# A transformer block with adaptive layer norm on one core: one of four x tiles loaded on two queues, and the 1 of the first scale added by TensorE

## The chip, the core and the metric

The kernel runs on one core of a Trainium2 chip. The metric is the device time of one execution in microseconds; runs of a kernel are compared by their median.

## What is computed

The inputs are bf16. x is 2 x 256 x 1152 (B, N, D), c is 2 x 1152, and the weights have D rows.

```python
def reference(x, c, wqkv, wo, w_mod):
    B, N, D = x.shape
    mod = (_silu(c) @ w_mod).reshape(B, 6, 1, D)
    shift_a, scale_a, gate_a, shift_m, scale_m, gate_m = [mod[:, i] for i in range(6)]
    h = _layernorm(x, axis=-1) * (1 + scale_a) + shift_a
    qkv = h @ wqkv
    ...
    p = _softmax(jnp.einsum('bqd,bkd->bqk', q, k) * D ** (-0.5), axis=-1)
    a = jnp.einsum('bqk,bkd->bqd', p, v) @ wo
    return x + gate_a * a
```

Three of the six parts of `mod` are used: the scale and the shift ahead of the projections, and the gate behind the output projection.

## The kernel before

The 512 tokens (both batches) lie in TT = 4 tiles of P = 128 rows, tiles 0 and 1 of the first batch and 2 and 3 of the second. D = 1152 is cut into KT = 9 blocks of 128.

**Layer norm in pieces.** Each x tile is centred by its mean (`centre`, into `xc`), and TensorE transposes the centred tile block by block (`transposes`, into the PSUM tiles `tp`); VectorE and ScalarE copy the result to `xcT` (`xcT_copy`). The division by the standard deviation comes later, so the K projection can begin before the variances are known. The mean of tile 0 comes from VectorE (`bn`), those of tiles 1 and 2 from sums on ScalarE (`act_mean`), that of tile 3 from both.

**Scale.** The scale row is silu(c) times a part of w_mod (`wS`). It is made in four column parts: PA (blocks 0 and 1), PB (2 to 4), PC (5 and 6), PD (7 and 8). For PA, `scale_rows` multiplies 128 x 128 blocks of `wS` with the replicated silu(c) (`scT_rep`, 32 columns) into the PSUM tile `psS`: 8 small matmuls for kk = 0 to 3 and 10 for kk = 4 to 8, each group behind a load of its own. Then `scale_out` adds 1 and writes `s1p` to SBUF, and `scaled` and `scaled_tp` multiply the transposed x by it into `hTs`.

**K projection.** `k_part`, `pair_part` and `k_step` accumulate wK against `hTs` in PSUM, block by block of k as the weights arrive: `acc` holds five of the nine output blocks, `psE` pairs of the others for the first two k, and `psK` the others for the rest. The shift (`wH`, into `psH`, by `shift_tiles`) is made after most of K, the third part of its weights last. Then come Q, the scores, V, the attention and the output projection.

**In front.** As x and the first weights arrive, TensorE runs `fillers(12)`: twelve matmuls of the constant tile `junk` (all ones, 512 columns) whose result nobody reads.

**Order.** Every engine's instructions run in the order in which they are written: lists for each engine are pinned at the end (`pin`). All large loads are issued on SP in a written order: x tiles 0, 1, 2, two loads of `wS` for PA, wK(0), x tile 3, wK(1), two loads of `wS` for PB, wK(2) to wK(4), and so on to `wH`, wQ, wG, wV and wO. ScalarE issues the small load of c on its own queue, and the last store. Each DMA takes one of eight semaphores in turn, and so waits for the DMA that had it before. Where nothing else is said, a DMA's landing is the sixteenth increment of its semaphore.

The change touches these lines of the main sequence (351, 366 to 372):

```python
    fillers(12)
    ...
    scale_rows(PA, 0, 4, where=BA)
    centre(2, nmean[:, 2:3], ALU.add)
    xcT_copy(1, 0, True)
    xcT_copy(1, 1, False)
    scale_rows(PA, 4, KT, js=[(0, 1), (1, 2)])
    scale_out(PA)
    scaled_b(0, 0)
    transposes(2, 0, BB)
```

`BA`, `BB` and `BC` name single PSUM banks; `scaled_b(0, 0)` is `scaled` for block 0 and the first batch. In the profile nearly all instructions stand under line 85, that of the helper that records them, so groups are told apart by their tiles.

Of the kernel before, what the change touches and what calls it, by code (L numbers as in the profile page):

```python
# [11 lines left out]
BF16 = mybir.dt.bfloat16  # L12
# [4 lines left out]
def kernel(  # L17
# [10 lines left out]
    P = 128  # L28
    B, N, D = x.shape
    T = B * N  # L30
    KT = D // P
# [9 lines left out]
    PA, PB, PC, PD = (0, 2), (2, 5), (5, 7), (7, KT)  # L41
    KA = PA[1]
    NR = 32

    x_f = x.rearrange("b n d -> (b n) d")
# [10 lines left out]
    const = ctx.enter_context(tc.tile_pool(name="const", bufs=1))  # L56
# [5 lines left out]
    MM, BA, BB, BC = (psum, "mm"), (psum_a, "pa"), (psum_b, "pb"), (psum_c, "pc")  # L62
# [3 lines left out]
    def bank(shape, name, dtype=None, where=None):  # L66
        if where is None:
            where = ring[turn_no[0] % len(ring)]
            turn_no[0] += 1
        return where[0].tile(shape, dtype or F32, tag=where[1], name=name)  # L70
# [21 lines left out]
    vec = _Rec(nc.vector, dve_seq)  # L92
    sca = _Rec(nc.scalar, act_seq)
    ten = _Rec(nc.tensor, pe_seq)
    spq = _Rec(nc.sync, sp_seq)
    gps = _Rec(nc.gpsimd, pool_seq)
# [10 lines left out]
    def tok(b):  # L107
        return slice(b * N, (b + 1) * N)

    def one(t):  # L110
        return slice(t * P, (t + 1) * P)

    junk = const.tile([P, 512], BF16)
# [4 lines left out]
        out=ident, in_=ident, compare_op=ALU.not_equal, fill=1.0, base=0,  # L118
# [9 lines left out]
        out=mask, in_=mask, compare_op=ALU.is_ge, fill=0.0, base=0,  # L128
# [3 lines left out]
        out=mask, in_=mask, compare_op=ALU.is_ge, fill=0.0, base=2,  # L132
# [2 lines left out]

    c_sb = const.tile([P, B, KT], BF16)
    x_sb = act.tile([P, TT, D], BF16)
    sca.preload_act_table_set("natural_log_exp_and_others")
    sca.dma_start(out=c_sb, in_=c.rearrange("b (p k) -> p b k", k=KT))

    wK = wpool.tile([P, KT, D], BF16)
    wQ = wpool.tile([P, KT, D], BF16, name="wQ")
# [4 lines left out]
    def load_x(t):  # L147
        spq.dma_start(out=x_sb[:, t, :], in_=x_f[t * P : (t + 1) * P, :])
# [4 lines left out]
    def load_s(part, k0, k1):  # L153
        load_mod(wS, 1, k0, k1, part[0] * P, part[1] * P)
# [10 lines left out]

    load_x(0)
    load_x(1)
    load_x(2)
    load_s(PA, 0, 4)
    load_s(PA, 4, KT)  # L170
    load_k(0, 1)
# [21 lines left out]
    def fillers(n):  # L193
        for _ in range(n):
            ten.matmul(junk_ps, lhsT=junk[:, :P], rhs=junk, start=True, stop=True)
# [7 lines left out]
    def sc_rhs(kk):  # L203
        return scT_rep[:, kk].rearrange("p r b -> p (r b)")
# [35 lines left out]
    def centre(t, scalar, op, c0=0, c1=D):  # L240
        vec.tensor_scalar(out=xc[:, t, c0:c1], in0=x_sb[:, t, c0:c1], scalar1=scalar, scalar2=None, op0=op)
# [4 lines left out]
    def transposes(t, h, where):  # L246
        k0, k1 = HALF[h]
        tp = bank([P, 5, P], "tp", BF16, where)
        for k in range(k0, k1):
            ten.transpose(tp[:, k - k0, :], xc[:, t, k * P : (k + 1) * P], ident)  # L250
        tps[t, h] = tp
# [9 lines left out]
    s1p = const.tile([P, KT, B], F32)  # L261
# [5 lines left out]

    psS = {}

    def scale_rows(part, kk0, kk1, js=None, where=None):  # L270
        if kk0 == 0:
            psS[part] = bank([P, part[1] - part[0], NR], "psS", where=where)
        for j0, j1 in [part] if js is None else js:
            for kk in range(kk0, kk1):
                for j in range(j0, j1):
                    ten.matmul(psS[part][:, j - part[0], :], lhsT=wS[:, kk, j * P : (j + 1) * P], rhs=sc_rhs(kk),
                               start=(kk == 0 and j == part[0]), stop=(kk == KT - 1), skip_group_check=True)

    def scale_out(part):
        vec.tensor_scalar_add(out=s1p[:, part[0] : part[1], :], in0=psS[part][:, :, 0:B], scalar1=1.0)  # L280
# [17 lines left out]
    def scaled(k, sl, scalar):  # L298
        vec.tensor_scalar(out=hTs[:, k, sl], in0=xcT[:, k, sl], scalar1=scalar, scalar2=None, op0=ALU.mult)
# [5 lines left out]
    def scaled_b(k, b):  # L305
        scaled(k, tok(b), s1p[:, k, b : b + 1])
# [41 lines left out]
        vec.tensor_tensor(out=qkT[:, KT + NACC + i, :], in0=psK[i], in1=held[:, i, :], op=ALU.add)  # L348


    fillers(12)
    sca.activation(out=e_sb, in_=c_sb, func=ACT.Exp, scale=-1.0)
    gps.tensor_scalar_add(out=e_sb, in0=e_sb, scalar1=1.0)
    bn(0, after_second=silu_c)
# [8 lines left out]
    xcT_copy(0, 1, False)  # L363
    transposes(1, 0, MM)
    transposes(1, 1, MM)
    scale_rows(PA, 0, 4, where=BA)
    centre(2, nmean[:, 2:3], ALU.add)
    xcT_copy(1, 0, True)
    xcT_copy(1, 1, False)
    scale_rows(PA, 4, KT, js=[(0, 1), (1, 2)])  # L370
    scale_out(PA)
    scaled_b(0, 0)
    transposes(2, 0, BB)
    transposes(2, 1, BC)
    scaled_tp(0, 2)
# [63 lines left out]
    def scale_part(part):  # L439
        scale_rows(part, 0, KT, where=BB)  # L440
        scale_out(part)
        for k in range(*part):
            for b in range(B):
                scaled_b(k, b)
# [112 lines left out]
    for b in range(B):  # L557
        s_ps = bank([P, NQ, N], "s_ps")
        for i in range(NQ):
            tq = b * NQ + i  # L560
            for k in range(KT):
                ten.matmul(s_ps[:, i, :], lhsT=qkT[:, k, tq * P : (tq + 1) * P], rhs=qkT[:, KT + k, tok(b)],
                           start=(k == 0), stop=(k == KT - 1))
# [75 lines left out]
    for b in range(B):  # L639
        for gi, dv0 in enumerate(range(0, KT, 2)):  # L640
            ndv = min(2, KT - dv0)
            ps = bank([P, 2, N], "ps")
            for dd in range(ndv):
                dv = dv0 + dd
                for j in range(NQ):
                    ten.matmul(ps[:, dd, :], lhsT=v_sb[:, b * NQ + j, dv * P : (dv + 1) * P],
                               rhs=pT_sbs[b][:, j, :], start=(j == 0), stop=(j == NQ - 1))
# [3 lines left out]
    for t in range(TT):  # L651
# [11 lines left out]
        for ci, (c0, w_) in enumerate(chunks):  # L663
# [6 lines left out]
            for k in range(KT):  # L670
                ten.matmul(
                    ps, lhsT=attnT[:, k, t * P : (t + 1) * P],
                    rhs=(wo_last[:, k, c0 - (D - TAILW) : c0 - (D - TAILW) + w_] if pregated else wO[:, k, cs]),
                    start=(k == 0 and not pregated), stop=(k == KT - 1),
# [49 lines left out]
```

## Time and profile before

| what | us |
|---|---|
| median of 3 runs (lowest, highest) | 96.11 (96.08, 96.26) |
| the profiled execution | 96.27 |
| its span, first to last instruction | 94.5 |
| TensorE busy (of the span) | 90.0 (95%) |
| VectorE busy | 69.9 (74%) |
| ScalarE busy | 34.3 (36%) |
| GpSimd busy | 20.4 (22%) |
| loads: bytes read from HBM | 19.76 MB |

PE is TensorE's matmul, PEld its weight load, DVE VectorE, ACT ScalarE, POOL GpSimd and SP the engine that issues the loads. A row of the timeline or of the chain begins with its start and its length in us; `<-` points from what an instruction reads to what it writes, and brackets give the idle time of the engine before it and what ended it. The rows of digits cut the span in 40 equal slices and give tenths. The ends of matmuls are modelled, so their starts are the surer figure.

### The profile page before, as it was taken

To read this page: it belongs to the slowest core of one execution; us is meant where nothing else is said; L and a number is where in the kernel's file an instruction comes from. 1 tells how busy PE (TensorE), PEld (TensorE's weight loads), DVE (VectorE), ACT (ScalarE), POOL (GpSimd) and SP (SyncE) were. 2 spreads that over 40 slices of the span, in tenths; PEclk is the share of its full clock that TensorE was granted. 3 is DMA by queue.
4 is the path that set the end of the run, shared out by engine and by line. 5 is a ranking of instruction groups with operands and counts; after the bars stand their busy time and mean duration, and the time that the engine had idled before them with its cause. 6 is when DMAs were issued, how large, how long until landed. Compare 5 with 4: busy or idle time off the path is not lost.

```text
span 94.5 us, 1687 instructions
## 1 busy us (share of the span) xinstructions
PE 90.0 (95%) x664; PEld 52.9 (56%) x664; DVE 69.9 (74%) x133; ACT 34.3 (36%) x71; POOL 20.4 (22%) x24
## 2 busy tenths in 40 slices
PE   3999999999999999999999999999999999999970
PEld 1349884543445444444468656565678665665660
DVE  2478889245898977999999899991018487889970
ACT  5198688002462700093420589234246300000010
POOL 5521000800000000000000000007999990002000
PEclk9999999999999999999999999999999999999999
DMA  1999999999999999999999702200000000302203
GB/s 25 321 275 378 373 400 358 365 393 407 398 410 412 411 410 412 401 375 365 380 410 411 285 18 56 54 9 0 0 0 0 0 0 7 125 34 91 105 26 118
DMA packets 17207, 21.31 MB, mean 225 GB/s; under 512 B 2224, under 2 KB 10544, under 8 KB 17200
## 3 DMA queue, kind: packets, MB, share of 16 engines
q1 hardware_dynamic: 16784, 21.17, 61.7%
q10 hardware_dynamic: 416, 0.04, 0.3%
q8 instruction: 5, 0.08, 0.3%
q14 instruction: 2, 0.02, 0.0%
HBM read 19.76 MB, written 1.18 MB: 222 GB/s over the span
## 4 chain that ended last, share of the span: by engine, by line
PE 93%; DVE 3%; issue 0%
PE ps L85 40%; PE psQ L85 18%; PE acc L85 11%; PE psK L85 7%; PE junk_ps L85 6%; PE s_ps L85 4%; PE psS L85 2%; PE tp L85 2%; PE psE L85 2%; PE psH L85 1%; DVE o_sb L85 1%; DVE ga L85 1%; DVE junk L85 1%; PE bc_ps L85 0%; DVE hTs L85 0%
## 5 line engine op out<-in xcount | busy, mean ns | idle before, releaser
L85 POOL PARTITION_ALL_REDUCE gate_bc<-gacc x2 | 13.7, 6886 | 45.2 <-DVE gacc L85 45.2
L85 DVE SCALAR_TENSOR_TENSOR gacc<-wG,scT_f,gacc 128x1152 f32<-128x1152 bf16 x16 | 22.4, 1416 | 0.4
L85 PE MATMUL ps<-wV,hT 128*128 128x384 bf16 x108 | 17.7, 326 | 0.0
L85 PE MATMUL psQ<-hT,wQ 128*128 128x512 bf16 x81 | 17.6, 379 | 0.0
L85 PE MATMUL ps<-wO,attnT 128*128 128x384 bf16 (+1 forms) x108 | 17.2, 322 | 0.0
L85 PEld LDWEIGHTS <-attnT 128*128 128x128 bf16 x117 | 11.1, 98 | 6.5
L85 PEld LDWEIGHTS <-hT 128*128 128x128 bf16 x108 | 10.6, 98 | 6.9
L85 PEld LDWEIGHTS <-wK 128*128 128x128 bf16 x109 | 9.3, 98 | 7.3 <-issue 0.6
L85 PEld LDWEIGHTS <-wQ 128*128 128x128 bf16 x81 | 7.9, 98 | 9.6
L85 PE MATMUL acc<-hTs,wK 128*128 128x512 bf16 (+2 forms) x65 | 11.3, 314 | 0.1
L85 ACT CAST qkT<-psQ 128x512 bf16<-128x512 f32 x9 | 4.9, 597 | 11.1 <-PE psQ L85 11.1
L85 DVE TENSOR_TENSOR ga<-ps,gate_bc 128x384 f32<-128x384 f32 (+1 forms) x12 | 6.5, 544 | 2.9 <-PE ps L85 2.9
L85 DVE CAST attnT<-ps 128x512 bf16<-128x512 f32 (+1 forms) x6 | 3.5, 603 | 6.8 <-PE ps L85 6.8
L85 ACT CAST v_sb<-ps 128x384 bf16<-128x384 f32 x12 | 5.5, 476 | 7.9 <-PE ps L85 7.9
L85 PE MATMUL psK<-hTs,wK 128*128 128x512 bf16 x28 | 6.9, 380 | 0.0
L85 DVE TENSOR_TENSOR o_sb<-ga,x_sb 128x384 bf16<-128x384 f32 (+1 forms) x12 | 6.6, 547 | 0.4
L85 PE MATMUL junk_ps<-junk 128*128 128x512 bf16 x12 | 5.3, 629 | 1.5 <-DVE junk L85 1.5
L85 ACT CAST o_sb<-ps 128x128 bf16<-128x128 f32 x1 | 0.3, 265 | 17.3 <-PE ps L85 17.3
L85 DVE TENSOR_TENSOR hT<-hTs,held 128x512 bf16<-128x512 bf16 x9 | 5.8, 686 | 0.9 <-ACT held L85 0.9
L85 DVE BATCH_NORM_STATS2 stats<-x_sb 128x6 f32<-128x384 bf16 x6 | 3.1, 542 | 2.3 <-DMA x_sb<-in_x_dram 2.3
L85 PEld LDWEIGHTS <-junk 128*128 128x128 bf16 (+1 forms) x13 | 1.7, 137 | 4.7 <-issue 3.2
L85 PE MATMUL s_ps<-qkT 128*128 128x256 bf16 x36 | 4.1, 272 | 0.0
(77 smaller groups left out, 84.6 us busy)
## 6 DMA issues: line engine op xcount, KB each, us to landing
wH<-in_w_mod_dram SPq DMA_DIRECT2D x3, 864.0 KB, 8.9
wG<-in_w_mod_dram SPq DMA_DIRECT2D x3, 864.0 KB, 12.3
wV<-in_wqkv_dram SPq DMA_DIRECT2D x3, 864.0 KB, 13.4
wO<-in_wo_dram SPq DMA_DIRECT2D x3, 864.0 KB, 8.8
wK<-in_wqkv_dram SPq DMA_DIRECT2D x7, 288.0 KB, 6.6
wQ<-in_wqkv_dram SPq DMA_DIRECT2D x3, 576.0 KB, 12.2
x_sb<-in_x_dram SPq DMA_DIRECT2D x4, 288.0 KB, 3.6
wS<-in_w_mod_dram SPq DMA_DIRECT2D x3, 320.0 KB, 7.6
```

The lines of the kernel that those rows point to most:

```text
L85: r = fn(*a, **k)
```

## The change

Tile 2 of x is loaded by two DMAs: rows 0 to 103 on SP, in the place of the whole tile, and rows 104 to 127 on ScalarE's queue behind c. One filler is left out. In its place `scale_open` opens the PSUM tile of part PA with a matmul of one row of ones against one row of ones, which writes 1 to each of its 64 columns; the scale matmuls of PA then accumulate on it. The first `scaled` reads its factor from `psS` itself, and `s1p` of PA is a plain copy, made after that `scaled`. The other parts are as before.

```diff
+    ones_row = const.tile([1, 2 * NR], BF16)
+    gps.memset(ones_row, 1.0)
     sca.preload_act_table_set("natural_log_exp_and_others")
     sca.dma_start(out=c_sb, in_=c.rearrange("b (p k) -> p b k", k=KT))
+    XS = 104
+    sca.dma_start(out=x_sb[XS:, 2, :], in_=x_f[2 * P + XS : 3 * P, :])
...
     load_x(0)
     load_x(1)
-    load_x(2)
+    spq.dma_start(out=x_sb[:XS, 2, :], in_=x_f[2 * P : 2 * P + XS, :])
     load_s(PA, 0, 4)
...
+    def scale_open(part, where):
+        n = part[1] - part[0]
+        psS[part] = bank([P, n, NR], "psS", where=where)
+        ten.matmul(psS[part].rearrange("p j r -> p (j r)"), lhsT=junk[0:1, :P], rhs=ones_row[0:1, 0 : n * NR],
+                   start=True, stop=False, skip_group_check=True)
+
     def scale_rows(part, kk0, kk1, js=None, where=None):
-        if kk0 == 0:
+        opened = part == PA
+        if kk0 == 0 and not opened:
             psS[part] = bank([P, part[1] - part[0], NR], "psS", where=where)
...
-                               start=(kk == 0 and j == part[0]), stop=(kk == KT - 1), skip_group_check=True)
+                               start=(kk == 0 and j == part[0] and not opened), stop=(kk == KT - 1),
+                               skip_group_check=True)
...
-    fillers(12)
+    fillers(11)
+    scale_open(PA, BA)
...
-    scale_rows(PA, 0, 4, where=BA)
+    scale_rows(PA, 0, 4)
...
     scale_rows(PA, 4, KT, js=[(0, 1), (1, 2)])
-    scale_out(PA)
-    scaled_b(0, 0)
+    scaled(0, tok(0), psS[PA][:, 0, 0:1])
+    vec.tensor_copy(out=s1p[:, PA[0] : PA[1], :], in_=psS[PA][:, :, 0:B])
     transposes(2, 0, BB)
```

## The prediction

> **What bounds the kernel now.** I read the engine rows and the slices of the page first, then the chain that ended last in order of time, then the front (5.7 to 9.1 us) instruction by instruction in the timeline, and last the stretches with their DMA share and the DMA queues. The page:
>
> ```profile
> PE 90.0 (95%) x664; PEld 52.9 (56%) x664; DVE 69.9 (74%) x133; ACT 34.3 (36%) x71; POOL 20.4 (22%) x24
> ...
> PEclk9999999999999999999999999999999999999999
> DMA  1999999999999999999999702200000000302203
> ```
>
> TensorE is busy from end to end, so the end moves only by what TensorE's stream gains or loses in its few holes. The DMA row is full through the first 22 slices (52 us). The change touches only the first 10 us of instructions, and the loads behind them. The chain there (start, length, what):
>
> ```profile
> 0.96 0.50 DVE junk L85
> 1.46 0.05 issue
> 1.51 5.30 PE junk_ps L85 x12
> 6.81 1.25 PE tp L85 x18
> 8.06 0.46 PE psS L85 x18
> 8.51 0.02 issue
> 8.54 0.17 DVE s1p L85
> 8.71 0.02 issue
> 8.73 0.30 DVE hTs L85
> 9.03 0.04 issue
> 9.07 0.98 PE acc L85 x10
> ```
>
> Twelve constant matmuls, eighteen transposes of tiles 0 and 1, the first scale part, the add of 1 (`s1p`), one scaling (`hTs`), then the K projection without a break. The timeline of the same stretch, then of two later holes:
>
> ```profile
> 6.21 0.11 PEld L85 LDWEIGHTS <-xc 128*128 128x128 bf16 x1 [0.32 <-DVE xc L85]
> ...
> 6.60 1.46 PE L85 MATMUL tp<-ident,xc 128*128 128x128 bf16 x18
> ...
> 8.54 0.16 DVE L85 TENSOR_SCALAR s1p<-psS 128x4 f32<-128x4 f32 x1
> ```
> ```profile
> 10.22 0.22 PEld L85 LDWEIGHTS <-wK 128*128 128x128 bf16 x3 [0.22 <-DMA wK<-in_wqkv_dram]
> ```
> ```profile
> 28.90 0.24 PEld L85 LDWEIGHTS <-scT_rep 128*32 128x32 bf16 x11 [0.17 <-issue]
> ```
>
> The first transpose's operand was there at 6.21 but its matmul started at 6.60, behind the last constant matmul. At 10.22 the weights for k=1 wait for their load. The hole at 28.90 has no releaser named; by the trace the third `wH` load landed at 28.855 and its first matmul started at 28.897. By the spacing of matmul starts, those two holes cost 0.107 and 0.131 us, and no other matmul after 9.1 us waits for a DMA. So the kernel is TensorE's stream held at two places by loads: **wK(1) at 10.2 and wH(third) at 28.9**.
>
> **The front, step by step.** Constant matmuls start 0.426 us apart, so without the twelfth TensorE is free at 6.175. The new one has 64 columns, 64/512 of that: 0.05 (an estimate from that spacing; between 0.03, the spacing of the 32-column psS matmuls, and 0.43), end 6.23. The operand was ready at 6.17, so the transposes start near 6.28, 0.32 earlier. The clock opened at 7.193: transposes are 0.107 apart before and 0.056 after. Eight and a half fit in 6.28 to 7.19, the other nine and a half take 0.53, so psS may start at 7.73, not 7.895. Its second half needs the wS load that landed at 7.95; before, TensorE got to it at 8.075. Now it waits there until about 8.00 and psS ends 8.42 instead of 8.50: 0.08 gained.
>
> Then `s1p` (8.538) goes from in front of the first `hTs` (8.734): 0.196 gained, `hTs` starts near 8.46. VectorE is free for it: `centre(2)` (7.61) waited for a copy that itself waited for the transposes, and can move to 7.40 (the mean is ready at 7.36), the copy after it to 7.83. Reading the factor from PSUM is not in the trace; the nearest row, the 128-column `hTs` from PSUM, takes 0.28 like the 256-column one from SBUF (0.29), so I take 0, and 0.1 as the other end (a gain has no reason). The copy of `s1p` now stands after the first `hTs`, at 8.66 to 8.82; queued behind it is `hTs` of tile 2, done at 9.14, and TensorE wants that only after five matmuls of 0.108, at 9.34: covered by 0.2. The first projection matmul moves from 9.075 to 8.80. **Sum: 0.27 at that point, and nothing at the end yet:** the 1.04 us of work up to wK(1) is then done at 9.84, while wK(1) landed at 10.175. The wait grows from 0.107 to 0.38. So the end is set by when wK(1), and then wH, land.
>
> Small edits, one answer each: `ones_row` (0.10, like the memset of `neg_half`) lies in GpSimd's idle 0.74 before `e_sb`. ScalarE's second DMA issue (0.45, like that of c) ends by 1.8, its next work starts at 3.90. On SP the semaphores shift by one: load_x(3) now waits for tile 0 (3.705, before its 3.857), wK(1)'s issue for tile 1 (4.47, so 0.14 later than its 4.33); it lands 5.8 us after issue behind loads already queued, so 0. From wK(2) on each waits for the same load as before. Tile 1 may land up to 0.18 later where two moved rows slip in front of it. ScalarE's sums start with it (4.47, 4.49), so the mean of tile 2 goes to 7.54, and `centre(2)` to 7.57, still before its old 7.61. Tile 0 late by as much would halve the 0.32.
>
> **The split load.** A 288 KB tile is 128 packets, eight on each of 16 DMA engines; the weight loads of that size landed 0.70 us apart, 0.088 a row. No load of the trace has 104 or 24 rows. Whole shares can leave an engine anything from none to 16 rows of this tile, so -0.70 to +0.70 us on an engine. I take the even shares, 13 engines with 8 and 12 with 2, because every load shown is cut evenly: twelve engines carry 10 rows (+0.18), one 8, three none (-0.70). The Trainium skill says the same of HWDGE transfers (DMA: Bandwidth & Descriptors, "Why a DMA increments its semaphore by 16 and not by 1"): the largest count up to 16 that divides the slowest dimension, on the lowest-numbered engines; no run so far shows it.
>
> Are the +0.18 seen? The stretches (PE, PEld, DVE, ACT, POOL, clock, DMA share, GB/s) and the queues of 13 to 30 us:
>
> ```profile
> 1.00:4.00 3.00, 2.49 (x6) 0.87 (x7) 0.72 (x2) 1.17 (x2) 2.06 (x5) 1.00 0.69 201
> 4.00:7.00 3.00, 3.00 (x11) 1.24 (x10) 2.52 (x7) 2.60 (x6) 0.96 (x3) 1.00 0.95 280
> 7.00:10.00 3.00, 2.94 (x55) 2.75 (x53) 2.61 (x10) 2.57 (x7) 0.24 (x1) 1.00 1.04 373
> ```
> ```profile
> q8 instruction: 2, 0.03, 0.7%
> ```
>
> Between 4 and 7 us the engines are filled to 0.95 where 1.04 follows: 0.27 us an engine unspent, more than two rows. The rows come on a second queue, behind c, just then. I take them as hidden (0), and keep +0.18 as the other end. For wK(1) the sixteen landings ran from 9.46 to 10.18, the four last at 10.06 or later; without the three relieved ones a landing near 10.05 is what I take: -0.12 at the first hole. For the third wH thirteen engines landed by 27.49 and three at 28.07, 28.79 and 28.86. One of the late ones fell 1.5 us behind right after a 16 KB instruction packet at 14.96, another after the one at 24.37: the instruction row. [...] The trace does not name the engines.
>
> **Sum:** -0.12 - 0.131 = -0.25. The profiled execution took 96.27 (span 94.5 and 1.77 around it), so 96.02; it stands 0.16 above the median, which becomes **95.86**. From -0.13 (second hole alone) to -0.33 (0.20 at the first).
>
> **Rivals.** *No change, 96.11:* the late engines of wH are not relieved, the two rows are hidden, and every front gain turns into a longer wait at 28.9. For it: that hole takes up any gain. Against: three late, three relieved. The Trainium skill speaks for this one too (same page, "Rules for kernel authors"): splitting a load over partitions and queues is not worth doing, as both parts share the same 16 engines; the even shares above would contradict it.
>
> *Slower, 96.29:* the twelve engines set the pace. Two rows of 0.088 are not hidden, wK(1) lands at 10.35 and the third wH at 29.03; TensorE waits for both and ends 0.18 later. It decides if the engine that lands last is one of the twelve and the early holes of the queues are not filled. For it: the DMA row is full for 52 us, so nothing is made up later; against: the 0.95.
>
> *Clock late, about 97.3:* a matmul less in front lets the clock open later than 7.19. TensorE's 2.6 us of work from there to 10.2 would at most double; less the 0.38 of waits and half of it again, +1.2. Against: transposes follow the filler without a hole. The Trainium skill (TensorE: Matmul & The Clock Gate, "The HAM clock gate") puts the next opening 3.4 us later if a window is missed; the trace has one opening and cannot show it.
>
> That the 1 is not added on TensorE, or the split not made, is excluded by the order of instructions, which shows both.
>
> **How the numbers follow.** Forecast 0.43, no change 0.24, slower by the twelve engines 0.28, clock 0.05. Range 95.75 to 96.36: the forecast's own is 95.78 to 95.98, the slower case's end 96.29 with 0.07 for a slower read from PSUM and a late tile 0; the clock case is left out. About 0.2% (0.19 us) is what a measurement here can tell from no change. The forecast's -0.25 passes it in a little over nine cases of ten; the slower case's +0.18 stands on it and passes in two of three. Faster 0.40, same 0.36, slower 0.24.
>
> **What would show it.** In the profile after: the first transpose near 6.3 and the first `acc` near 8.8; the wait for wK(1) longer than 0.22, ending near 10.05 if the rows are hidden, 10.35 if not; no hole in front of the third part of `psH` if the late engines are the relieved ones. A first `acc` later than 9.07, or transposes still 0.107 apart after 7.2, would break the front; a wH landing at 28.86 or later breaks the forecast.

## The result: 0.46 us slower, where 0.25 faster was forecast

The changed kernel takes 96.58 us (median of 20 runs, 96.44 to 96.89) against 96.12 (20 runs, 95.87 to 96.65): a ratio of 1.0042, 95% interval 1.0026 to 1.0058. The forecast of 95.86 had the wrong sign, and 96.58 lies above its range. The profiled execution of the changed kernel took 96.51, with a span of 94.8.

The page of the changed kernel shows TensorE busy 1.0 us less than before, the clock full, and the DMA row full through the first 22 slices:

```profile
PE 89.0 (94%) x664; PEld 52.6 (55%) x664; DVE 70.0 (74%) x133; ACT 34.1 (36%) x71; POOL 20.5 (22%) x25
...
PEclk9999999999999999999999999999999999999999
DMA  2999999999999999999999502110000000302203
```

TensorE does less work and ends later, so something holds it. The chain that ended last names it (changed kernel, start, length, what). Before the change this chain ran on TensorE from its first constant matmul on, with `s1p` and one `hTs` as its only steps elsewhere in the front; now it does not touch TensorE until 11.73:

```profile
1.25 3.81 DMA x_sb<-in_x_dram
...
5.08 1.26 ACT xc L85 x2
...
6.47 1.25 ACT xc L85 x2
7.74 0.21 ACT nmean L85
...
7.98 0.52 DVE xc L85
8.50 0.34 DVE xcT L85
...
8.94 0.29 DVE hTs L85
9.23 0.08 DVE s1p L85
...
9.41 0.67 DVE hTs L85 x3
10.08 0.20 DVE xcT L85
10.28 0.60 DVE half L85
...
11.23 0.37 DVE xc L85
11.59 0.14 issue
11.73 0.38 PE tp L85 x4
```

It begins with the load of tile 1 (3.81 us from its issue), goes over ScalarE's sums of tiles 1 and 2 (`xc` on ACT) to the mean of tile 2 at 7.95, over VectorE's `centre(2)`, the copy of tile 1, the four `hTs` with `s1p` among them, the copy of tile 2 and the half sum of tile 3, to the centring of tile 3 and its first transpose. The timeline of the changed kernel gives the two waits in it, and TensorE's starts in front:

```profile
5.08 1.16 ACT L85 ACTIVATE xc<-x_sb 128x1152 bf16<-128x1152 bf16 x1 [0.90 <-DMA x_sb<-in_x_dram]
...
6.20 0.68 PE L85 MATMUL tp<-ident,xc 128*128 128x128 bf16 x9 [0.61 <-DVE xc L85]
...
9.28 0.98 PE L85 MATMUL acc<-hTs,wK 128*128 128x256 bf16 x10
...
11.73 0.38 PE L85 MATMUL tp<-ident,xc 128*128 128x128 bf16 x4 [0.20 <-DVE xc L85]
```

The same two starts before:

```profile
4.49 1.16 ACT L85 ACTIVATE xc<-x_sb 128x1152 bf16<-128x1152 bf16 x1 [0.37 <-DMA x_sb<-in_x_dram]
...
11.28 0.39 PE L85 MATMUL tp<-ident,xc 128*128 128x128 bf16 x4
```

ScalarE's first sum starts at 5.08 where it started at 4.49; the first `acc` starts at 9.28, not at 9.07 as before or 8.80 as forecast; and tile 3's first transpose stands at 11.73, not at 11.28. From there to the first `psH` TensorE loses nothing more: 28.46 against 28.01, again 0.45. The span grew by less, 94.8 against 94.5, since the hole of 0.131 at the third `wH` was in before's profiled execution and is not in this one. That execution lay 0.15 above its kernel's median, so the two medians, 0.46 apart, are what the 0.45 is to be held against. Nothing behind tile 3 moves: in all nineteen profiled executions of this document the time from its first transpose to the end is 84.78 to 84.87, but for before's 85.00 with that hole.

The stretch of 4 to 7 us, with TensorE, its weight loads, VectorE, ScalarE, GpSimd, clock, DMA share and GB/s, in which I had counted on 0.27 us an engine of unspent DMA time:

```profile
4.00:7.00 3.00, 2.26 (x16) 1.04 (x14) 2.47 (x7) 2.07 (x5) 0.96 (x3) 1.00 1.08 289
```

The share rose from 0.95 to 1.08, by 14%, and the bytes from 280 to 289 GB/s, by 3%. The engines were busier, but with longer packets: rows of 2304 bytes, 0.093 us each on an undisturbed engine, took 0.155 on average between 4.50 and 5.00.

### The profile page after: what moved, and what is told of

Same layout as the page of the kernel before. It is cut to its first block, busy times and chain, and to the rows that moved or that the text cites. A ratio compares the mean times of both kernels' runs of the same rounds, so it can differ in the third digit from the quotient of the medians.

```text
span 94.8 us, 1692 instructions
## 1 busy us (share of the span) xinstructions
PE 89.0 (94%) x664; PEld 52.6 (55%) x664; DVE 70.0 (74%) x133; ACT 34.1 (36%) x71; POOL 20.5 (22%) x25
## 4 chain that ended last, share of the span: by engine, by line
PE 83%; DVE 5%; DMA 4%; ACT 3%; issue 1%; SPq 0%; DVEq 0%
PE ps L85 40%; PE psQ L85 18%; PE acc L85 9%; PE psK L85 7%; PE s_ps L85 4%; DMA x_sb<-in_x_dram 4%; ACT xc L85 3%; PE psS L85 1%; PE psE L85 1%; PE psH L85 1%; DVE o_sb L85 1%; DVE hTs L85 1%; DVE ga L85 1%; DVE xc L85 1%; PE tp L85 1%
## 5 line engine op out<-in xcount | busy, mean ns | idle before, releaser
L85 PE MATMUL junk_ps<-junk 128*128 128x512 bf16 x11 | 4.0, 532 | 1.5 <-DVE junk L85 1.5
L85 PE MATMUL tp<-ident,xc 128*128 128x128 bf16 x36 | 2.9, 220 | 1.4 <-DVE xc L85 1.4
L85 PE MATMUL ps<-pT,v_sb 128*128 128x256 bf16 x36 | 4.1, 272 | 0.0
```

Source lines behind the costliest of these rows:

```text
L85: r = fn(*a, **k)
```

## The experiments

"Tile 1 lands" is the sixteenth increment of its load, "mean" the end of ScalarE's mean of tile 2, "tile 3" the start of its first transpose; all come from the profiled execution of the kernel named. Before has 4.47, 7.36 and 11.28; the changed kernel 5.05, 7.95 and 11.73. The theory after the comparison: the 24 rows on ScalarE's queue make tile 1 late, and `s1p`, in its new place, lengthens VectorE's work behind that. The rivals: one of the two halves of the change does it all; the uneven shares of 104 and 24 rows do it; the slip is in tile 2 itself.

### The halves

**The edits without the split.** The changed kernel with tile 2 loaded whole on SP:

```diff
-    XS = 104
-    sca.dma_start(out=x_sb[XS:, 2, :], in_=x_f[2 * P + XS : 3 * P, :])
...
-    spq.dma_start(out=x_sb[:XS, 2, :], in_=x_f[2 * P : 2 * P + XS, :])
+    load_x(2)
```

> The three TensorE and VectorE edits alone (one filler less, the 1 added on TensorE, the copy of s1p behind the first hTs); tile 2 of x whole on SP. If the split load is what costs: tile 1 lands near 4.47 us as before, the wait behind tile 3's chain is gone, and the time is that of before or a little less, 95.95 to 96.15. If the edits cost by themselves (the copy of s1p holds up VectorE, the filler is missed): 96.4 to 96.6 with tile 1 on time.

Measured: 96.11 against 96.15, ratio 1.0004 (0.9985 to 1.0023). Tile 1 lands at 4.43. The timeline of this kernel:

```profile
8.46 0.29 DVE L85 TENSOR_SCALAR hTs<-xcT,psS 128x256 bf16<-128x256 bf16 x1
...
8.80 0.98 PE L85 MATMUL acc<-hTs,wK 128*128 128x256 bf16 x10
...
10.19 1.05 PEld L85 LDWEIGHTS <-wK 128*128 128x128 bf16 x12 [0.39 <-DMA wK<-in_wqkv_dram]
```

and the piece of its chain that follows:

```profile
4.25 5.91 DMA wK<-in_wqkv_dram
10.15 0.04 issue
10.20 0.72 PE acc L85 x5
```

The first `hTs` at 8.46 and the first `acc` at 8.80 are the forecast's numbers to the hundredth. The 0.39 is the idle time of the weight loads; by the spacing of matmul starts, in which the forecast's 0.38 was worked out, TensorE waits 0.27 for wK(1), and 0.09 just before it, at `psE`, behind ScalarE's copy of tile 2. The front gains 0.27 and gives it all back there: alone, these edits do nothing to the time that can be told.

**The split without the edits.** Before, with tile 2 as 104 rows on SP and 24 on ScalarE's queue behind c:

```diff
+    XS = 104
+    sca.dma_start(out=x_sb[XS:, 2, :], in_=x_f[2 * P + XS : 3 * P, :])
...
-    load_x(2)
+    spq.dma_start(out=x_sb[:XS, 2, :], in_=x_f[2 * P : 2 * P + XS, :])
```

> The split load alone (104 rows on SP, 24 on ScalarE's queue behind c), all else as before. If the split costs: tile 1 lands near 5.0, tile 2 near 6.1, the mean of tile 2 is ready near 7.9 instead of 7.36, and the time is 96.4 to 96.7. If the edits are the cause: 96.0 to 96.15.

Measured: 96.39 against 96.15, ratio 1.0022 (0.9995 to 1.0049). Tile 1 lands at 5.20, mean at 8.09, tile 3 at 11.66. The tile that was not touched is late by 0.73. In this execution wK(1) landed late too, at 10.56 (fifteen of its sixteen increments were there by 9.80), and TensorE's wait for it put tile 3 at 11.66, some 0.05 after VectorE was ready. In time the loss is about half of the change's and at the edge of what can be told.

**Both again, in one comparison.** The changed kernel and the split alone, once more on one chip:

> The changed kernel once more, on the same chip as the split alone, to tell whether the edits cost or gain beside the split. If the copy of s1p behind the first hTs costs on VectorE's late chain (0.07 us by the spacing of hTs): 0.05 to 0.2 above the split alone. If the edits are covered: the same within 0.1.

> The split alone once more: 96.35 to 96.5 by its first run, tile 1 at 5.0 to 5.2 if its lateness was not of one execution.

Measured, against 96.22: the changed kernel 96.64, ratio 1.0034 (1.0007 to 1.0060); the split alone 96.38, ratio 1.0009 (0.9983 to 1.0034). Tile 1 lands at 5.09 and 5.07, mean at 7.99 and 7.97, tile 3 stands at 11.86 and 11.49. Not all of these 0.37 are the edits'. In the first execution the second load of `wS` and wK(1) also landed late (8.57 and 10.74, against 7.91 and 10.19 in the other): the first `hTs` waited 0.09 more, and TensorE waited for wK(1) and was ready for tile 3 only 0.01 ahead of VectorE. The cleaner pair is the changed kernel's first profile and this one of the split alone: mean at 7.95 and 7.97, tile 3 at 11.73 and 11.49, and in both TensorE waits for VectorE. As times, the medians differ by 0.26 here and by 0.19 in the first pair (96.58, 96.39). The intervals against before overlap, but the runs themselves part: of the twelve runs each on this chip none of the changed kernel is below 96.48, and seven of the split alone are below 96.40; in 124 of the 144 pairs the changed kernel is the slower. So the edits that were free alone cost about 0.2 beside the split.

### `s1p`, and the order on VectorE

**`s1p` behind the copy of tile 2.** All four `hTs` of PA read `psS`, and the copy comes after them, once on the changed kernel and once on the edits alone:

```diff
-    vec.tensor_copy(out=s1p[:, PA[0] : PA[1], :], in_=psS[PA][:, :, 0:B])
...
-    scaled_tp(0, 2)
-    scaled_b(1, 0)
-    scaled_tp(1, 2)
+    for k in range(KA):
+        if k:
+            scaled(k, tok(0), psS[PA][:, k, 0:1])
+        vec.tensor_scalar(out=hTs[:, k, one(2)], in0=tps[2, 0][:, k, :], scalar1=psS[PA][:, k, 1:2],
+                          scalar2=None, op0=ALU.mult)
     xcT_copy(2, 0, True, skip=KA)
+    vec.tensor_copy(out=s1p[:, PA[0] : PA[1], :], in_=psS[PA][:, :, 0:B])
```

> The changed kernel, with all four first scalings of VectorE reading their factor from PSUM and the copy of s1p behind the copy of tile 2's transposes. If VectorE's chain down to tile 3's transposes is what carries the late tile 1 to TensorE: the second hTs follows the first by 0.2 instead of 0.47 us, tile 3's first transpose starts near 11.55 instead of 11.73, and the time is 96.35 to 96.45. If the end follows the load of wK alone: 96.58 as it is.

> The edits without the split, with that same order of VectorE. Tile 1 near 4.45. If VectorE's chain sets tile 3's transposes, they start near 11.1 instead of 11.25 and the time is 95.9 to 96.05; if the wait for wK(1) sets them, 96.1.

Measured: on the changed kernel 96.54, ratio 1.0044 (1.0017 to 1.0072); on the edits alone 96.24, ratio 1.0008 (0.9980 to 1.0035). As times, a miss: nothing was gained. The profile says why for the first. In that execution tile 2 itself was late too (ScalarE's sum of it waited until 6.75, against 6.47), so the mean came at 8.24, 0.29 after the changed kernel's. From the mean to tile 3's first transpose it took 3.59, where the changed kernel took 3.78 and 3.87 (with the 0.09 of late `wS`). The order of the copy is worth about 0.2 in that chain; the later tile took it away. That it would show in the time with equal loads is not shown.

**ScalarE late, the loads on time.** Before, with an activation in front of ScalarE's sum of tile 1:

```diff
+    late = small.tile([P, 512], BF16, tag="late", name="late")
+    sca.activation(out=late, in_=x_sb[:, 1, 0:512], func=ACT.Copy)
```

> The kernel before with all loads as they were, and one more ScalarE instruction ahead of tile 1's sum (a copy of 512 columns of tile 1 to a scratch tile, some 0.5 us). If the late tile 1 reaches the end through ScalarE's two sums and VectorE's chain alone: the mean of tile 2 near 7.9 instead of 7.36, tile 3's first transpose 11.4 to 11.6 instead of 11.28, 96.2 to 96.4. If the end follows the loads: 96.1.

Measured: 96.34, ratio 1.0004 (0.9976 to 1.0032). Tile 1 lands at 4.41, its sum starts at 4.97, the mean ends at 7.82 and tile 3 stands at 11.35. The mean 0.46 later moved tile 3 by 0.07 only: before has slack there. The time is inconclusive.

### What makes tile 1 late

**Both parts on SP.** Before, with the two parts of tile 2 one behind the other on the load queue:

```diff
-    load_x(2)
+    XS = 104
+    spq.dma_start(out=x_sb[:XS, 2, :], in_=x_f[2 * P : 2 * P + XS, :])
+    spq.dma_start(out=x_sb[XS:, 2, :], in_=x_f[2 * P + XS : 3 * P, :])
```

> As the split alone, but both parts on SP, the 24 rows behind the 104. If slipping in front of tile 1 on a second queue is what delays: tile 1 at 4.47 as before, tile 2 about 0.2 later than 5.72, 96.1 to 96.25. If uneven shares slow the packets themselves: tile 2 lands at 6.1 or later, 96.3 to 96.6.

**Extra rows, tile 2 whole.** Before, with the 24 rows loaded a second time on ScalarE's queue, into a tile that nobody reads:

```diff
+    again = const.tile([P, D], BF16, name="again")
+    sca.dma_start(out=again[104:, :], in_=x_f[2 * P + 104 : 3 * P, :])
```

> The kernel before, all of x on SP as it was, and 24 rows of tile 2 loaded once more on ScalarE's queue behind c, into a tile that nobody reads (55 KB more in all). If rows that go in front of tile 1 on the second queue make the whole delay: tile 1 at 5.0 to 5.2 us, 96.3 to 96.45. If half of it comes from slow packets of the uneven 104-row load: tile 1 near 4.7, 96.1 to 96.25.

Measured: both parts on SP 96.23, ratio 1.0006 (0.9984 to 1.0028); extra rows 96.34, ratio 1.0022 (0.9999 to 1.0044). ScalarE's sum of tile 1 in the first, then in the second:

```profile
4.56 1.16 ACT L85 ACTIVATE xc<-x_sb 128x1152 bf16<-128x1152 bf16 x1 [0.49 <-DMA x_sb<-in_x_dram]
```
```profile
5.19 1.16 ACT L85 ACTIVATE xc<-x_sb 128x1152 bf16<-128x1152 bf16 x1 [1.14 <-DMA x_sb<-in_x_dram]
```

The uneven parts behind tile 1 on its own queue leave it at 4.54. The rows on the second queue, with tile 2 uncut, put it at 5.17. So it is not the cut: 24 rows issued after tile 1 on another queue, and moved beside it, are enough. Nor is it the long rows: here they took 0.098 on average between 4.50 and 5.00, not 0.155, and tile 1 was as late.

**More and fewer rows on the second queue.** Before with the split at 112, 80 and 120 rows, the rest on ScalarE's queue; the diff is that of the split with another `XS`.

> As the split alone, but 112 rows on SP and 16 on ScalarE's queue, which divide evenly over 16 engines (7 and 1). If uneven shares (13 and 12 engines) are what delays: tile 1 by 4.6, tile 2 by 5.8, 96.1 or less. If rows on a second queue slip in front of tile 1: tile 1 at 4.6 to 4.9 (16 rows instead of 24), 96.2 to 96.45.

> The split alone, at 80 rows on SP and 48 on ScalarE's queue: 5 and 3 rows on each of 16 engines. If only the number of rows in front counts (3 instead of 2): tile 1 at 5.1 or later, 96.35 to 96.6. If uneven shares make the packets slow: packets of 0.093 us throughout, tile 1 at 4.7 to 4.9 (three rows of 0.088), tile 2 by 5.8, 96.1 to 96.2.

> The split alone at 120 rows on SP and 8 on ScalarE's queue (one row on each of eight engines). If the delay grows with the rows on the second queue (0.42 at 16, 0.6 to 0.7 at 24): tile 1 near 4.7, 96.1 to 96.2. If any x rows on the second queue bring the whole delay: tile 1 at 5.0 or later, 96.35 to 96.5.

Measured: 16 rows 96.12, ratio 0.9986 (0.9957 to 1.0016), tile 1 at 4.89; 48 rows 96.50, ratio 1.0034 (1.0009 to 1.0058), tile 1 at 5.08; 8 rows 96.36, ratio 1.0024 (0.9990 to 1.0058), tile 1 at 4.75. In the six profiles with no rows beside tile 1 it landed at 4.38 to 4.54, so a slip of 0.1 is scatter. The slip grows from 0.28 over 0.42 to 0.6 or 0.7 at 24 rows, and not further at 48. The loads of 16 and 48 rows show sixteen increments each, so their shares are even, and uneven ones are not needed for the slip. The profiled execution with 8 rows took 95.96, the shortest of its twelve, with tile 3 at 11.17, earlier than before's; the median, with an interval that holds 1, stays open. 16 rows cost no time that can be told and gain none.

**The rows elsewhere.** The 24 rows on SP between tiles 0 and 1; the 24 rows on ScalarE's queue ahead of c; tile 1 cut in the place of tile 2, its own last 24 rows behind c:

```diff
     load_x(0)
+    XS = 104
+    spq.dma_start(out=x_sb[XS:, 2, :], in_=x_f[2 * P + XS : 3 * P, :])
     load_x(1)
-    load_x(2)
+    spq.dma_start(out=x_sb[:XS, 2, :], in_=x_f[2 * P : 2 * P + XS, :])
```
```diff
+    XS = 104
+    sca.dma_start(out=x_sb[XS:, 2, :], in_=x_f[2 * P + XS : 3 * P, :])
     sca.dma_start(out=c_sb, in_=c.rearrange("b (p k) -> p b k", k=KT))
...
-    load_x(2)
+    spq.dma_start(out=x_sb[:XS, 2, :], in_=x_f[2 * P : 2 * P + XS, :])
```
```diff
     sca.dma_start(out=c_sb, in_=c.rearrange("b (p k) -> p b k", k=KT))
+    XS = 104
+    sca.dma_start(out=x_sb[XS:, 1, :], in_=x_f[P + XS : 2 * P, :])
...
-    load_x(1)
+    spq.dma_start(out=x_sb[:XS, 1, :], in_=x_f[P : P + XS, :])
```

> The split alone, but the 24 rows are issued on SP between tile 0 and tile 1, so that they stand in front of tile 1 on its own queue and nothing but c is on ScalarE's. If rows in front cost what their number says (two rows of 0.088 on twelve engines): tile 1 near 4.65, 96.1 to 96.2. If 24 rows in front delay tile 1 by 0.6 on any queue: tile 1 near 5.1, 96.35 to 96.45.

> The split alone, with the 24 rows ahead of c on ScalarE's queue. If the lateness comes from two queues that both carry x: tile 1 at 5.0 to 5.2 as with c first, and c a little later, 96.35 to 96.5. If it comes from the rows standing behind c's many small packets: tile 1 near 4.65, 96.1 to 96.25.

> The kernel before, with tile 1 split 104 and 24 instead of tile 2: the rows on ScalarE's queue now belong to the tile that is needed first. If rows of another tile in front of tile 1 are the harm: tile 1 lands at 4.3 to 4.6 us, tile 2 near 5.8, 96.0 to 96.2. If any rows on the second queue beside SP's, or the uneven shares, are the harm: tile 1 at 4.9 or later, 96.3 to 96.5.

Measured: between the tiles on SP 97.30, ratio 1.0119 (1.0084 to 1.0154); ahead of c 97.09, ratio 1.0088 (1.0056 to 1.0120); tile 1 cut 96.82, ratio 1.0054 (1.0025 to 1.0084). ScalarE's sum of tile 1 starts at 6.49, 5.75 and 5.82. Each is worse than the change, and longer than either of its expectations. For the third the theory of the slip had expected otherwise, and missed. With the rows ahead of c it is not tile 1 alone: c landed at 5.60 (before 3.88), `e_sb` on ScalarE, ahead of the sum, waited for it, tile 0 landed at 4.34 (before 3.71) and tile 1 at 5.38. And with the rows between the tiles tile 1 slips by 2.0 on one queue alone, so a second queue is not needed for harm; why it is so much is not settled. Wherever rows join the first loads, a load beside or behind them pays.

**Rows spread, and half rows.** The extra rows once written to every fifth partition, and once as half rows to the old 24 partitions; each kernel ran once beside before:

```diff
+    again = const.tile([P, D], BF16, name="again")
+    sca.dma_start(out=again[0:120:5, :], in_=x_f[2 * P + 104 : 3 * P, :])
```
```diff
+    again = const.tile([P, D], BF16, name="again")
+    sca.dma_start(out=again[104:, : D // 2], in_=x_f[2 * P + 104 : 3 * P, : D // 2])
```

> Kernel before with 24 extra rows on ScalarE's queue behind c, written to every fifth partition of a spare tile (0 to 115), where the earlier run wrote them to partitions 104 to 127; x whole on SP, nothing reads them. Theory A (what counts is that rows of 2304 bytes are queued and in flight in front of tile 1 on the second queue): tile 1 lands at 5.0 to 5.2 again, against 4.47 before, and the first hTs starts at 9.0 or later. Rival B (the rows are slow since they all go to the same few partitions): tile 1 lands at 4.7 or earlier and the first hTs starts at 8.8 or earlier. The earlier run had 5.17 and 9.05.

> Kernel before with 24 extra half rows (576 of 1152 columns) on ScalarE's queue behind c, to partitions 104 to 127 of a spare tile; x whole on SP, nothing reads them. By bytes: 27 KB in front of tile 1 is half of the earlier run's 54 KB, so about half of its +0.70: tile 1 lands near 4.8. By the number of rows put between those of the load queue: as many as there, tile 1 at 5.0 to 5.2.

Measured: spread 96.61 and half rows 96.17, before 96.11. ScalarE's two sums with the spread rows:

```profile
4.42 1.16 ACT L85 ACTIVATE xc<-x_sb 128x1152 bf16<-128x1152 bf16 x1 [0.40 <-DMA x_sb<-in_x_dram]
6.41 1.16 ACT L85 ACTIVATE xc<-x_sb 128x1152 bf16<-128x1152 bf16 x1 [0.50 <-DMA x_sb<-in_x_dram]
```

The spread load took 1.31 to issue, not 0.69, and 21 of its 24 rows moved after 3.75 (of the earlier extra rows 13), beside tile 2: tile 1 is on time at 4.40, and tile 2 lands at 6.39, 0.67 after before's 5.72. Without foreign rows it landed at 5.72 to 6.10 (before, edits alone with either place of `s1p`, ScalarE late), so its slip is 0.3 to 0.7. Tile 1's landing is the rival's number; the first `hTs` at 9.19 looks like the theory's, but its scale matmuls waited 0.38 for the second load of `wS`, so it does not decide. That the slip has moved to the next tile, and needs no crowd on a few partitions, is likely from this one profile and not shown. Half rows put tile 1 at 4.68, a slip of 0.21 where whole rows gave 0.70; one profile, which speaks for the bytes and against the number of rows.

### Where the 0.58 is

The trace lists the packets. Each load of a tile has sixteen of 4 bytes behind its rows, the load of 24 rows twelve; from these counts I take them as the increments being sent. For tile 1, with the median of the sixteen packets and of the sixteen increments that the semaphore shows:

| kernel | rows beside tile 1 | packets | increments | apart | tile 1 lands |
|---|---|---|---|---|---|
| before | none | 3.97 | 4.30 | 0.34 | 4.47 |
| edits alone | none | 3.90 | 4.21 | 0.31 | 4.43 |
| both parts on SP | none | 3.91 | 4.30 | 0.39 | 4.54 |
| 120/8 | 8 | 4.01 | 4.47 | 0.46 | 4.75 |
| half rows | 24 halves | 3.97 | 4.43 | 0.46 | 4.68 |
| 112/16 | 16 | 3.89 | 4.35 | 0.46 | 4.89 |
| 80/48 | 48 | 4.03 | 4.61 | 0.58 | 5.08 |
| extra rows, spread | 24, later | 3.80 | 4.14 | 0.34 | 4.40 |
| extra rows | 24 | 4.16 | 4.83 | 0.67 | 5.17 |
| split alone | 24 | 4.13 | 4.80 | 0.67 | 5.20 |
| split alone, again | 24 | 4.10 | 4.84 | 0.74 | 5.07 |
| the change | 24 | 4.10 | 4.82 | 0.72 | 5.05 |
| the change, again | 24 | 4.13 | 4.90 | 0.77 | 5.09 |

The packets come 0.14 to 0.19 later with 24 rows: the two rows in front of them, as sized. The rest, 0.33 to 0.43, lies between the packet and its increment; with 48 rows, three on each engine, it is 0.24, so it does not simply grow with the rows. The Trainium skill (DMA: Bandwidth & Descriptors, in the paragraph on HWDGE ordering) says that an increment is a strongly ordered write, which lands only after every earlier write of that engine, across its queues. The trace agrees that increments wait longer when another queue's rows are in flight. By that rule alone the twelve engines that carry those rows would be late; in the trace all sixteen increments are, the earliest at 4.57 instead of 4.01. What the writes share and wait for is not settled.

## Why the prediction was wrong, point by point

**The step that failed: "Tile 1 may land up to 0.18 later where two moved rows slip in front of it."** It landed 0.58 later. 0.18 was the time that two rows occupy an engine, and that term was right for the packets; the term for what comes behind them, 0.33 to 0.43, was missing. With it fell the next sentence, `centre(2)` at 7.57 "still before its old 7.61": it started at 7.98, and the first `acc`, forecast for 8.80, at 9.28. The 0.27 of unspent DMA time was read as room; the share shows busy time, not when a write is done.

**The second: the copy of `s1p` was "covered by 0.2".** I asked when TensorE wants the next `hTs` (9.34) and not who stands behind `s1p` on VectorE. From the first `hTs` to the second is 0.20 before (8.73 to 8.94) and 0.47 after (8.94 to 9.41), and all that follows moves with it. The second one before:

```profile
8.94 0.28 DVE L85 TENSOR_SCALAR hTs<-tp,s1p 128x128 bf16<-128x128 bf16 x1
```

From the first `hTs` to the end of the first half of tile 3's centring VectorE takes 2.37 to 2.39 in the fourteen profiles with `s1p` in front of it, 2.64 in the three with `s1p` right behind it, and 2.45 or 2.46 in the two with `s1p` behind the copy of tile 2. Wherever TensorE waits there, tile 3's first transpose starts 0.15 after that end.

The whole chain from the mean of tile 2 to that transpose is 3.52 or 3.53 where nothing else waits (the split alone again, the other splits of tile 2 on two queues, the extra rows), 3.78 in the change and 3.59 with `s1p` behind; it is longer where the first `hTs` waits for `psS`, or TensorE for wK(1). Before used 3.91, so a late mean had 0.39 of slack.

**A limit that the prediction left out.** Of that slack only 0.02 lies behind the first `hTs`: before, tile 3's centring ends at 11.10, the transpose could start at 11.25 and started at 11.28. So VectorE came to tile 3 just ahead of TensorE, and the prediction, which looked for loads alone, has no such place. In the edits alone VectorE gains 0.27 at the first `hTs` and loses it at the copy of `s1p`; its centring ends at 11.09. An earlier wK(1) could then bring 0.03 (an estimate from these distances), not the forecast's 0.12. The edits with `s1p` behind bear it out: wK(1) landed at 9.97, and TensorE waited 0.15 for VectorE at tile 3.

**The sum with the measured terms.** The mean is 0.58 later (7.95 against 7.36). Less the 0.39 of slack that leaves 0.19; the split alone, with its mean 0.61 later, showed 0.22 (11.49 against 11.28). The longer chain adds 0.26 (3.78 less 3.52). Together 0.45 at tile 3, with no place to make it up behind it; the medians are 0.46 apart. By the constant 84.8 behind tile 3 the medians 96.58 and 96.12 stand for a transpose at about 11.8 and 11.3 (an estimate). The kernels follow this place through to the time:

| kernel (times of its profiled execution; medians from several chips, before 96.12 to 96.22) | mean of tile 2 | tile 3 | first `psH` | us, this execution | us, median |
|---|---|---|---|---|---|
| 120/8 | 7.64 | 11.17 | 27.90 | 95.96 | 96.36 |
| edits alone | 7.44 | 11.25 | 27.99 | 96.08 | 96.11 |
| before (with the hole) | 7.36 | 11.28 | 28.01 | 96.27 | 96.12 |
| 112/16 | 7.79 | 11.31 | 28.05 | 96.11 | 96.12 |
| ScalarE late | 7.82 | 11.35 | 28.08 | 96.18 | 96.34 |
| split alone, again | 7.97 | 11.49 | 28.23 | 96.28 | 96.38 |
| extra rows | 8.06 | 11.59 | 28.32 | 96.40 | 96.34 |
| split alone | 8.09 | 11.66 | 28.40 | 96.46 | 96.39 |
| the change | 7.95 | 11.73 | 28.46 | 96.51 | 96.58 |
| the change, again | 7.99 | 11.86 | 28.59 | 96.68 | 96.64 |
| tile 1 cut | 8.69 | 12.21 | 28.95 | 96.99 | 96.82 |
| rows ahead of c | 8.60 | 12.23 | 28.97 | 97.02 | 97.09 |
| rows between tiles on SP | 9.36 | 12.89 | 29.62 | 97.69 | 97.30 |

The medians follow more loosely than the executions, 120/8 most of all: tile 3 itself moves from execution to execution.

**The hole at the third `wH`.** The 0.131 was to vanish because the split relieves the late engines. No run shows that term: which engines the late ones are, and which the 104 rows leave out, no trace names. The third `wH` landed at 28.86 there, at 28.36 with the edits alone (no split), and at 28.32 and 28.84 in the two profiles of the change, so one kernel spans nearly the whole difference; three engines were late in the first three of these too. One other profile shows a hole there, of 0.04 (the edits with `s1p` behind, `wH` at 28.69). A term of half the forecast's gain rested on a single landing.

**wK(1).** It was sized at 10.05 after the split; it landed at 9.85 and 10.74 in two profiles of the change, 10.56 and 10.19 in two of the split alone and 10.15 in the edits alone. The execution moves it more than the edit does. In the first profile of the change nothing waited for it; in the second TensorE waited 0.25.

**What held.** The filler, the matmul of ones and the read of the factor from PSUM (0.29 per `hTs`, as from SBUF) are as worked out; the edits alone show 8.46, 8.80 and the end of `psS` at 8.42. The shares are even: the counter of the 24 rows shows 12 increments from its engines, that of the 104 rows 13. By the Trainium skill's rule on the count, given with the prediction, it had to be so, and here the trace agrees.

**The rivals.** No change, 96.11, is what the edits alone did, for the reason that every gain became a longer wait, at wK(1) though and not at `wH`. The rule of the Trainium skill named beside it (DMA: Bandwidth & Descriptors, "Rules for kernel authors"), that such a split is not worth doing, pointed the right way; its reason, that both parts share the engines, gives no loss, and the trace shows one. The slower rival had the right sign by another mechanism: in the first profile of the change wK(1) and `wH` landed earlier than in its 10.35 and 29.03, and the time was lost all the same. In the second wK(1) was later than 10.35, by 0.39, but VectorE alone would have held tile 3 at the same 11.86. The clock opened in time: the transposes at 6.20 already ran 0.056 apart.

## What to carry to other kernels

Before a small transfer is put on a second queue, look at which earlier transfers are still in flight when its rows move, and ask who waits for their last increment: the price is paid by a load that the edit does not touch, and it can be several times the rows' own time. When an instruction is moved on an in-order engine, cost it against the whole queue behind it and against the slack of that queue's last user, not only against the next reader. Where two engines reach one instruction within 0.02 of each other, moving one of them forward gains nothing. A hole seen in one profiled execution is a gain only if other executions have it too.

## What was not expected of the hardware

The increment of a load stood 0.31 to 0.39 behind its packet when its rows were alone, and 0.67 to 0.77 with 24 foreign rows moving beside them. The clock opened at 7.19 in before's profile, 4.38 in the change's, and between 4.2 and 7.5 in the others, with no tie to the time that the profiles show; the transposes of tile 0 ran 0.107 or 0.056 apart accordingly. A load of 24 rows took 0.69 on ScalarE's queue to issue, and 1.31 when it wrote to every fifth partition, against 0.42 for a whole tile on SP.
